# Queries and keys on both halves of the partitions: transposes on parts of the array in an attention and MLP kernel

## The chip, the cores and the metric

The kernel runs on one core of a Trainium2 chip. Its time is the device time of one execution in microseconds (us), beside it the profile of one more execution. The core has five engines that run side by side, each through its own instructions in order: TensorE (PE; its weight loads are PEld), VectorE (DVE), ScalarE (ACT), GpSimd (POOL) and SyncE (SP). POOL and SP issue all DMA transfers here. TensorE computes `out = in.T @ moving` with `in` as weights, and transposes by taking the tile as weights and an identity matrix as the moving operand. Results of TensorE lie in PSUM until VectorE or ScalarE copies them to SBUF.

## The reference

Inputs are q, k and v of 8 batches, 8 heads, 576 tokens, 64 values (float32), and two matrices `moe_w_in` (512 x 2048) and `moe_w_out` (2048 x 512). Per batch and head:

```python
scores = scale * np.matmul(q, k.transpose(0, 1, 3, 2))
mask_plain = (rel >= 0) & (rel < window)                 # heads 0 to 3, window 32
mask_dil = (rel >= 0) & (rel < window * dilation) & (rel % dilation == 0)   # heads 4 to 7, dilation 4
attn = softmax(where(mask, scores, -1e9));  out = attn @ v
x = out as (4608 tokens, 512);  h = x @ w_in;  result = silu(h) @ w_out
```

`rel` is the distance from a key's position to the query's. A query sees 32 keys: the last 32 positions, or every fourth of the last 128.

## The kernel before, in words

**Attention.** Heads come in two kinds, `z = 0` (heads 0 to 3, plain) and `z = 1` (heads 4 to 7, dilated). Scores and values work on blocks of 32 queries and 64 keys. For scores, q and k must lie transposed, head dimension on the partitions. For `z = 0` two heads share the 128 partitions (`qT`, `kT`). For `z = 1` the tokens are sorted into four classes (position modulo 4), and two neighbouring tokens, that is two classes, share the partitions (`qC`, `kC`).

**Loading.** `load_qk` (L89) brings q and k of one batch in by POOL, cast to f16, in four transfers: heads 0 to 3 of k and of q, then heads 4 to 7 of k and of q. Partition p holds the tokens 8p to 8p + 7 of every head, so 72 partitions are in use. Batch 0 has a loader (`load_qk0`) and a transposer (`transpose0`) of its own, in two parts of the sequence.

**Transposing batches 1 to 7.** For `z = 0`, `pair` (L236) first copies two heads side by side on VectorE, so that one token's values of both heads are 128 neighbouring columns. `transpose` (L244) then makes eight transposes (one per token in the row) of 72 rows by 128 columns into one PSUM tile, and one copy sorts the result into `qT` or `kT`. For `z = 1` no pairing is needed, since two neighbouring tokens are neighbours in memory: `transpose_classes` (L257) makes eight transposes of the same size. For k the copy out of PSUM is made by VectorE, for q by ScalarE (`both`, L645). PSUM tiles with the tag `ps` rotate through four buffers.

**The MLP.** `layer1` (L590) makes 16 blocks of hidden units, each of 8 matmuls (288 columns), with SiLU on ScalarE; batch 0 does it in two parts (`layer1_part`). `layer2` (L623) makes 4 or 5 output tiles of 16 matmuls (512 columns).

**The order.** The schedule is written out by hand. `plan_of(b)` (L668) puts the attention work of later batches into batch b's MLP: `at(step, function, ...)` runs a function ahead of block `step` of layer 1 (0 to 15) or of a group of four matmuls of layer 2 (16 and up); negative steps belong to the first part of batch 0. The transposes of a batch and kind are made in two bursts, each for two head pairs' worth of one step: in batches 2 and later, `z = 1` of batch b + 1 at steps 2 and 6, `z = 0` of batch b + 2 at steps 12 and 14, with the pair copies at 9 and 10, and scores follow at steps 10 and 17. `load_qk(b + 3)` is issued at step 8. In the start, POOL's order is: q and k of batch 0, v of batch 0, `w_in`, q and k of batch 1, `w_out`, the clearing of a v buffer, v of batch 1, q and k of batch 2. SyncE shifts v of batch 1 (`shift_v`) from step 14 of batch 0 on.

## Time and profile before

| | |
|---|---|
| median of 3 runs | 344.65 us (343.04 to 346.63) |
| the profiled execution | 345.1 us, of which the span of instructions is 343.3 us |
| granted TensorE clock | 1.0 throughout |
| TensorE busy | 320.1 us (93%), 4824 matmuls |
| VectorE busy | 194.1 us (57%) |
| ScalarE busy | 216.6 us (63%) |
| POOL busy | 76.4 us (22%) |
| layer 1 of batches 1 to 7 (L595) and layer 2 (L631) | 119.1 + 132.2 us of TensorE |
| transposes of batches 1 to 7 (L253, L262) | 224 of `z = 0` and 224 of `z = 1`, in 28 bursts of 16 |
| q and k transfers of batches 1 to 7 (L96) | 28 of 288 KB |

How to read the profile: an operation's line names the engine, the line of the kernel, what it writes and reads, its shape (for TensorE rows*columns of the weights first) and its count. Matmuls are pipelined: the length of one includes its way through the array, so the distance between starts tells what it costs. A row of slices shows 40 equal slices of the span, each digit the busy share in tenths. The chain of waits follows the last instruction back to what released it.

### The profile page before, as it was taken

Reading aid. Unit: us, or ns where it says so; the run is one execution under the profiler, and the core shown is the slowest. Engines: PE = TensorE matmul, PEld = TensorE weight load, DVE = VectorE, ACT = ScalarE, POOL = GpSimd, SP = SyncE. Lnnn points to the kernel's source line nnn. Section 1 sums busy time; section 2 is a strip of 40 time slices with the busy share of each in tenths; the row PEclk is TensorE's granted clock in tenths of the full one; section 3 lists DMA queues with packets and bytes.
Section 4 is the critical chain, followed back from the end, with each engine's and each line's share of the span. In section 5 each row is a group of like instructions: output and inputs, shape, how many; then the busy total and the mean of one; then the engine's idle time right before and its main releaser. Section 6 shows DMA issues by size and latency. Waiting matters only on the chain.

```text
span 343.3 us, 11208 instructions
## 1 busy us (share of the span) xinstructions
PE 320.1 (93%) x4824; PEld 209.5 (61%) x4824; DVE 194.1 (57%) x438; ACT 216.6 (63%) x746; POOL 76.4 (22%) x120
## 2 busy tenths in 40 slices
PE   4549998799999999999899999999999999999995
PEld 4437863377744677467655677458755677457642
DVE  7776575866667755855656456655756443440021
ACT  2693669046799556976499356986599356916400
POOL 8835543254200450044001530023000000000000
PEclk9999999999999999999999999999999999999999
DMA  6999999989911596158802946039002100110021
GB/s 85 165 215 189 202 190 179 215 155 113 144 62 50 94 128 101 63 77 121 138 7 89 161 80 96 33 82 137 10 5 91 63 2 3 61 63 2 0 83 71
DMA packets 49089, 32.84 MB, mean 96 GB/s; under 512 B 24112, under 2 KB 43568, under 8 KB 49040
## 3 DMA queue, kind: packets, MB, share of 16 engines
q0 software_dynamic: 42848, 21.74, 47.6%
q1 hardware_dynamic: 6192, 10.39, 9.2%
q8 instruction: 37, 0.61, 0.7%
q14 instruction: 12, 0.10, 0.1%
HBM read 37.75 MB, written 9.44 MB: 137 GB/s over the span
## 4 chain that ended last, share of the span: by engine, by line
PE 73%; DMA 16%; ACT 3%; DVE 3%; issue 2%; POOL 1%; SPq 0%; POOLq 0%
PE h L595 33%; PE o L631 28%; DMA w_out<-in_moe_w_out_dram 5%; DMA vw<-in_v_dram 4%; PE x L507 3%; ACT pe L446 3%; DMA vw<-vw 3%; DMA w_in<-in_moe_w_in_dram 2%; PE pt L471 2%; DMA qn<-in_q_dram 2%; PE t L253 2%; PE t L262 2%; DVE pn L462 1%; PE s L306 1%; PE s L294 1%
## 5 line engine op out<-in xcount | busy, mean ns | idle before, releaser
L631 PE MATMUL o<-w_out,gT 128*128 128x512 f16 x576 | 132.2, 380 | 0.0
L603 ACT ACTIVATE gT<-h 128x576 f16<-128x576 f32 x112 | 72.8, 650 | 85.0 <-PE h L595 85.0
L595 PE MATMUL h<-xT,w_in 128*128 128x288 f16 x896 | 119.1, 287 | 1.3 <-issue 1.3
L595 PEld LDWEIGHTS <-w_in 128*128 128x128 f16 x896 | 84.4, 98 | 23.5 <-issue 1.7
L446 ACT ACTIVATE pe<-ms,nm 128x64 f32<-128x64 f32 x284 | 94.2, 334 | 3.3 <-DVE nm L375 3.2
L631 PEld LDWEIGHTS <-gT 128*128 128x128 f16 x576 | 53.8, 98 | 58.0
L639 DVE COPY ob<-o 128x512 f32<-128x512 f32 x36 | 24.8, 689 | 59.1 <-PE o L631 59.1
L446 ACT ACTIVATION_READ_ACCUMULATOR pe<-ms,nm 128x1 f32 x284 | 53.2, 187 | 0.0
L402 DVE SCALAR_TENSOR_TENSOR ms<-s,mask 128x512 f32<-128x512 f32 x28 | 19.2, 686 | 26.3 <-PE ss L294 17.6
L119 POOL DMA_DIRECT2D vw<-in_v_dram x16 | 10.2, 639 | 103.1 <-PE xs L564 98.6
L586 DVE CAST xT<-x 128x256 f16<-128x256 f32 x56 | 21.1, 418 | 12.4 <-PE xs L553 8.2
L462 DVE TENSOR_TENSOR pn<-pe,r 128x640 f16<-128x640 f32 (+2 forms) x32 | 25.3, 792 | 1.1
L418 DVE TENSOR_REDUCE nm<-ms 128x10 f32<-128x640 f32 (+1 forms) x28 | 22.0, 786 | 1.0
L479 DVE COPY ptT<-pt 128x640 f16<-128x640 f16 (+2 forms) x32 | 15.0, 470 | 11.5 <-PE pt L471 11.5
L614 PE MATMUL h<-xT,w_in 128*128 128x256 f16 (+1 forms) x128 | 19.4, 304 | 0.8 <-DVE xT L543 0.8
L269 DVE COPY kC<-t 128x576 f16<-128x576 f16 (+2 forms) x18 | 12.3, 686 | 12.2 <-PE t L262 12.2
L471 PE MATMUL pt<-ident,pn 128*128 128x128 f16 x152 | 14.7, 229 | 4.5 <-DVE pn L462 4.5
L621 ACT ACTIVATE gT<-h 128x512 f16<-128x512 f32 (+1 forms) x16 | 10.4, 650 | 11.6 <-PE h L614 11.6
L471 PEld LDWEIGHTS <-pn 128*128 128x128 f16 x152 | 10.1, 101 | 12.1 <-DVE pn L462 9.7
L507 PEld LDWEIGHTS <-vw 64*64 64x64 f16 x896 | 9.7, 109 | 11.2 <-issue 10.0
L255 DVE COPY kT<-t 128x576 f16<-128x576 f16 x14 | 10.5, 754 | 8.3 <-PE t L253 8.3
L614 PEld LDWEIGHTS <-w_in 128*128 128x128 f16 x128 | 12.5, 103 | 4.3 <-issue 0.8
(82 smaller groups left out, 288.9 us busy)
## 6 DMA issues: line engine op xcount, KB each, us to landing
out_dram<-ob SPq DMA_DIRECT2D x36, 256.0 KB, 2.0
kn<-in_k_dram POOLq DMA_DIRECT2D x14, 288.0 KB, 8.6
qn<-in_q_dram POOLq DMA_DIRECT2D x14, 288.0 KB, 9.1
vw<-in_v_dram POOLq DMA_DIRECT2D x8, 288.0 KB, 6.7
vw<-in_v_dram POOLq DMA_DIRECT2D x16, 128.0 KB, 3.6
w_in<-in_moe_w_in_dram POOLq DMA_DIRECT2D x4, 512.0 KB, 12.0
w_out<-in_moe_w_out_dram POOLq DMA_DIRECT2D x4, 512.0 KB, 17.2
vw<-vw POOLq DMA_DIRECT2D x12, 128.0 KB, 2.7
```

Source lines behind the costliest of these rows:

```text
L402: nc.vector.scalar_tensor_tensor(out=ms[:, 0:8].rearrange("p (n t) c -> p n (t c)", n=2), in0=s[hi].rearrange("p n t c -> p n (t c)"), sca ...
L418: nc.vector.tensor_reduce(out=nm[:, 0:w], in_=ms[:, 0:w], axis=AX.X, op=ALU.max, negate=True)
L446: nc.scalar.activation(pe[:, t, :], ms[:, t, :], AF.Exp, bias=nm[:, t : t + 1], accum_out=l[:, t : t + 1],)
L462: nc.vector.tensor_tensor(pn[:, 0:w], a["pe", z, hi][:, 0:w], r[:, 0:w, None].broadcast_to([P, w, KB]), ALU.mult)
L471: nc.tensor.transpose(t[:, i, :], a["pn", z, hi][:, 2 * i : 2 * i + 2].rearrange("p t c -> p (t c)"), ident)
L507: nc.tensor.matmul(dst, w, p, start=True, stop=True)
L586: copy(f(xT[:, 2 * z + n, 0:NS]), f(a["x", z][n]))
L595: nc.tensor.matmul(h[:, half, 0:HS], w_in16[:, c, f * P : f * P + P], xT[:, c, half * HS : half * HS + HS], start=(c == 0), stop=(c == MC ...
L603: nc.scalar.activation(gT[:, f, s0 : s0 + S].rearrange("p (a c) -> p a c", a=2), h[:, :, 0:HS], AF.Silu)
L614: nc.tensor.matmul(h[:, i, 0 : c1 - c0], w_in16[:, c, (f + i) * P : (f + i + 1) * P], xT[:, c, c0:c1], start=(c == 0), stop=(c == MC - 1),)
L631: nc.tensor.matmul(o, gT[:, f, t * P : (t + 1) * P], w_out16[:, f, :], start=(f == 0), stop=(f == NFF - 1),)
L639: nc.vector.tensor_copy(ob, o)
```

## The change

- `load_qk` puts the heads of a batch on both halves of the partitions. For `z = 0`, heads 0 and 1 lie on partitions 0 to 63 and heads 2 and 3 on 64 to 127, with 9 tokens per partition. For `z = 1`, heads 4 and 5 lie on partitions 0 to 47 and heads 6 and 7 on 64 to 111, with 12 tokens per partition. There are eight transfers per batch (two heads each) in place of four, `z = 1` ahead of `z = 0`.
- `pair` and its buffers are gone.
- `transpose` now makes a burst for all four heads of a kind of q or of k. For `z = 0` it has 9 x 2 x 2 = 36 transposes of 64 rows by 64 columns, each on a quarter of the array: the half of the partitions gives the rows, the head within the pair the columns. For `z = 1` it has 6 x 2 x 2 = 24 transposes of 48 rows by 128 columns, on a half of the array. The two halves write two PSUM tiles; both are copied out at the end of the burst, one by VectorE and one by ScalarE.
- The steps of the bursts stay; one burst is for k and the next one for q, where each had one head pair's k and q before. Batch 0 keeps its transposes in parts, in tiles of the new names.

```diff
+HF = P // 2
+URS = (9, 12)
     def load_qk(b):
-        qk[b] = (
-            nat.tile([UP, H, UR, D], F16, tag="qn", name=f"qn_{b}"),
-            nat.tile([UP, H, UR, D], F16, tag="kn", name=f"kn_{b}"),
-        )
-        for h0 in (0, HH):
-            for dst, src in ((qk[b][1], k), (qk[b][0], q)):
-                nc.gpsimd.dma_start(
-                    out=dst[:, h0 : h0 + HH],
-                    in_=src[b, h0 : h0 + HH].rearrange("h (p u) d -> p h (u d)", u=UR),
-                )
+        for which in (0, 1):
+            t = nat.tile([P, H * UR, D], F16, tag=f"n{which}", name=f"n{which}_{b}")
+            u0, u1 = 2 * URS[0], 2 * (URS[0] + URS[1])
+            qk[b, 0, which] = t[:, 0:u0].rearrange("p (h u) d -> p h u d", h=2)
+            qk[b, 1, which] = t[:, u0:u1].rearrange("p (h u) d -> p h u d", h=2)
+        for z in (1, 0):
+            for which, src in ((1, k), (0, q)):
+                for i in (0, 1):
+                    h = 2 * (2 * z + i)
+                    nc.gpsimd.dma_start(
+                        out=qk[b, z, which][i * HF : i * HF + UPS[z]].rearrange("p h u d -> p h (u d)"),
+                        in_=src[b, h : h + 2].rearrange("h (p u) d -> p h (u d)", u=URS[z]),
+                    )
...
-    def pair(b, hp, which):
-        a = att(b)
-        p = a["pair", hp, which] = prp.tile([UP, UR, 2, D], F16, tag="pair", name=f"p{which}_{b}_{hp}")
-        nc.vector.tensor_copy(
-            p, qk[b][which][:, 2 * hp : 2 * hp + 2].rearrange("p h u d -> p u h d")
-        )
-    def transpose(b, hp, which, copy=nc.vector.tensor_copy):
...
+    def transpose(b, z, which, copies):
+        a = att(b)
+        src, n, ur = qk[b, z, which], UPS[z], URS[z]
+        ts = [ps.tile([P, ur, n], F16, tag="ps", name=f"t{which}_{b}_{z}_{i}") for i in (0, 1)]
+        for u in range(0, ur, 1 + z):
+            for h in (0, 1):
+                for i in (0, 1):
+                    r = slice(i * HF, i * HF + n)
+                    if z == 0:
+                        dst, w = ts[i][h * D : h * D + D, u, :], src[r, h, u, :]
+                    else:
+                        dst = ts[i][:, u // DIL * 4 + 2 * h + u % DIL // 2, :]
+                        w = src[r, h, u : u + 2, :].rearrange("p u d -> p (u d)")
+                    nc.tensor.transpose(dst, w, ident[r, r])
+        for i in (0, 1):
+            if z == 0:
+                o = (a["qT"][:, i], a["kT"][:, i, W:])[which]
+                copies[i](o.rearrange("d (p u) -> d p u", u=ur), ts[i].rearrange("d u p -> d p u"))
+            else:
+                to_classes(a, which, i, 0, ts[i].rearrange("d (e m) p -> d e m p", m=4), copies[i])
...
-    both = (nc.scalar.copy, nc.vector.tensor_copy)
+    both = (nc.vector.tensor_copy, nc.scalar.copy)
+    def transposes(at, b, z, steps):
+        for n in (0, 1):
+            at(steps[n], transpose, b, z, 1 - n, both)
...
-            transposes(at, 1, 0, (1, 1, 3, 3), (-2, -2, -1, -1))
+            transposes(at, 1, 0, (1, 3))
...
-                transposes(at, b + 1, 1, (2, 2, 6, 6))
+                transposes(at, b + 1, 1, (2, 6))
...
-                transposes(at, b + 2, 0, (12, 12, 14, 14), (9, 9, 10, 10))
+                transposes(at, b + 2, 0, (12, 14))
```

More of the change, by code (lines that the diff above doesn't have):

```diff
@@ L46 @@
     CL = S // DIL
-    UP = S // UR
+    UPS = [S // u for u in URS]
     HS = S // 2
@@ L51 @@
     PA = SA // UR
+    PB = (S - SA) // UR
     WM = 12
@@ L57 @@
     nat = ctx.enter_context(tc.tile_pool(name="nat", bufs=2))
-    prp = ctx.enter_context(tc.tile_pool(name="prp", bufs=4))
     msp = ctx.enter_context(tc.tile_pool(name="msp", bufs=5))
@@ L89, in load_qk, with load_qk0 @@
     def load_qk(b):
-        qk[b] = (
-            nat.tile([UP, H, UR, D], F16, tag="qn", name=f"qn_{b}"),
-            nat.tile([UP, H, UR, D], F16, tag="kn", name=f"kn_{b}"),
-        )
-        for h0 in (0, HH):
-            for dst, src in ((qk[b][1], k), (qk[b][0], q)):
-                nc.gpsimd.dma_start(
-                    out=dst[:, h0 : h0 + HH],
-                    in_=src[b, h0 : h0 + HH].rearrange("h (p u) d -> p h (u d)", u=UR),
-                )
-    def load_qk0(part, halves):
-        t0, n = ((0, PA), (SA, UP - PA))[part]
-        if part not in qk0:
-            qk0[part] = (
-                nat.tile([UP, H, UR, D], F16, tag="qn", name=f"qn_0{part}"),
-                nat.tile([UP, H, UR, D], F16, tag="kn", name=f"kn_0{part}"),
-            )
+        for which in (0, 1):
[11 more added lines that the diff above has]
+                    )
+    def load_qk0(part, halves):
+        t0, n = ((0, PA), (SA, PB))[part]
+        if part not in qk0:
+            qk0[part] = [
+                nat.tile([P, H * UR, D], F16, tag=f"n{i}", name=f"n{i}_0{part}").rearrange(
+                    "p (h u) d -> p h u d", h=H
+                )
+                for i in (0, 1)
+            ]
         for h0, h1 in halves:
@@ L160, in class_v @@
         return a["vw"][e * KB : e * KB + KB, NP + j // 2 * ND + h * DIL + r]
-    qk = [None] * B
+    qk = {}
     qk0 = {}
@@ L234, in att @@
         return state[b]
-    def pair(b, hp, which):
+    def transpose(b, z, which, copies):
         a = att(b)
-        p = a["pair", hp, which] = prp.tile([UP, UR, 2, D], F16, tag="pair", name=f"p{which}_{b}_{hp}")
-        nc.vector.tensor_copy(
-            p, qk[b][which][:, 2 * hp : 2 * hp + 2].rearrange("p h u d -> p u h d")
-        )
-    def transpose(b, hp, which, copy=nc.vector.tensor_copy):
-        a = att(b)
-        if hp >= HP // 2:
-            return transpose_classes(b, qk[b][which], 0, UP, hp, which, copy)
-        t = ps.tile([P, UR, UP], F16, tag="ps", name=f"t{which}_{b}_{hp}")
-        p = a.pop(("pair", hp, which))
-        for u in range(UR):
-            nc.tensor.transpose(t[:, u, :], p[:, u], ident[:UP, :UP])
-        o = (a["qT"][:, hp], a["kT"][:, hp, W:])[which]
-        copy(o.rearrange("d (p u) -> d p u", u=UR), t.rearrange("d u p -> d p u"))
@@ L257, in transpose_classes @@
-    def transpose_classes(b, src, i0, n, hp, which, copy):
-        a = att(b)
-        t = ps.tile([P, UR // DIL, 4, UP], F16, tag="ps", name=f"t{which}_{b}_{hp}_{i0}")[:, :, :, 0:n]
-        for h in (0, 1):
-            for u in range(0, UR, 2):
-                nc.tensor.transpose(
-                    t[:, u // DIL, 2 * h + u % DIL // 2, :],
-                    src[0:n, 2 * hp + h, u : u + 2, :].rearrange("p u d -> p (u d)"),
-                    ident[0:n, 0:n],
-                )
-        dst, off = ((a["qC"], 0), (a["kC"], W))[which]
-        h0, i0 = 2 * hp - HH, off + i0
+        src, n, ur = qk[b, z, which], UPS[z], URS[z]
@@ new lines, in transpose, with to_classes @@
+        for i in (0, 1):
[4 more added lines that the diff above has]
+                to_classes(a, which, i, 0, ts[i].rearrange("d (e m) p -> d e m p", m=4), copies[i])
+    def to_classes(a, which, i, t0, t, copy):
+        e, n = t.shape[1], t.shape[3]
+        dst, i0 = ((a["qC"], 0), (a["kC"], W))[which]
+        i0 += t0 // DIL
@@ L269, in transpose_classes @@
         copy(
-            dst[:, h0 : h0 + 2, :, i0 : i0 + n * UR // DIL].rearrange("d h r (p e) -> d (h r) p e", e=UR // DIL),
+            dst[:, 2 * i : 2 * i + 2, :, i0 : i0 + n * e].rearrange("d h r (p e) -> d (h r) p e", e=e),
             t.rearrange("d e m p -> d m p e"),
@@ L277, in transpose0 @@
         src = qk0[part][which]
-        t0, n = ((0, PA), (SA, UP - PA))[part]
+        t0, n = ((0, PA), (SA, PB))[part]
+        t = ps.tile([P, UR, n], F16, tag="ps", name=f"t{which}_0{part}_{hp}")
         if hp >= HP // 2:
-            return transpose_classes(0, src, t0 // DIL, n, hp, which, copy)
-        t = ps.tile([P, UR, UP], F16, tag="ps", name=f"t{which}_0{part}_{hp}")[:, :, 0:n]
+            t = t.rearrange("d (e m) p -> d e m p", m=4)
+            for h in (0, 1):
+                for u in range(0, UR, 2):
+                    nc.tensor.transpose(
+                        t[:, u // DIL, 2 * h + u % DIL // 2, :],
+                        src[0:n, 2 * hp + h, u : u + 2, :].rearrange("p u d -> p (u d)"),
+                        ident[0:n, 0:n],
+                    )
+            return to_classes(a, which, hp - HP // 2, t0, t, copy)
         for u in range(UR):
@@ L641, in layer2 @@
             nc.sync.dma_start(out=out[row : row + P, :], in_=ob)
-    both = (nc.scalar.copy, nc.vector.tensor_copy)
-    def transposes(at, b, z, steps, pairs=None):
-        for n in range(4):
-            hp, which = 2 * z + n // 2, 1 - n % 2
-            if z == 0:
-                at(pairs[n], pair, b, hp, which)
-            at(steps[n], transpose, b, hp, which, both[which])
+    both = (nc.vector.tensor_copy, nc.scalar.copy)
+    def transposes(at, b, z, steps):
+        for n in (0, 1):
+            at(steps[n], transpose, b, z, 1 - n, both)
     def later(at, b, z, steps):
@@ L693, in plan_of @@
             at(-3, last_finish, 0, 0, 1)
-            transposes(at, 1, 0, (1, 1, 3, 3), (-2, -2, -1, -1))
+            transposes(at, 1, 0, (1, 3))
             at(5, scores, 1, 0)
-            transposes(at, 1, 1, (7, 7, 9, 9))
+            transposes(at, 1, 1, (7, 9))
             at(10, load_qk, 3)
@@ L710, in plan_of @@
             at(0, shift_v, 3, nc.gpsimd, (ALL,))
-            transposes(at, 2, 0, (2, 2, 4, 4), (0, 0, 2, 2))
-            transposes(at, 2, 1, (8, 8, 10, 10))
-            transposes(at, 3, 0, (14, 14, 15, 15), (11, 11, 12, 12))
+            transposes(at, 2, 0, (2, 4))
+            transposes(at, 2, 1, (8, 10))
+            transposes(at, 3, 0, (14, 15))
             at(6, scores, 2, 0)
```

## The prediction

> **What bounds the kernel now.** I read the page first: the engines' busy time, the row of slices and the chain.

> ```profile
> PE 320.1 (93%) x4824; PEld 209.5 (61%) x4824; DVE 194.1 (57%) x438; ACT 216.6 (63%) x746; POOL 76.4 (22%) x120
> ...
> PE   4549998799999999999899999999999999999995
> ...
> PE 73%; DMA 16%; ACT 3%; DVE 3%; issue 2%; POOL 1%; SPq 0%; POOLq 0%
> ```

> TensorE is busy in nearly every slice after the first four. The answer by stretches sharpens that: from 113 to 306 us it is idle for 1.6 us of 193, while VectorE, which the change relieves, is idle for 81.

> ```profile
> 113.00:306.00 193.00, 191.39 (x2905) 125.09 (x2897) 112.37 (x252) 132.89 (x453) 31.33 (x48) 1.00 0.41 74
> ```

> Then the waits of TensorE, to see whom it waits for. After 25 us there are few: for the softmax rows `pn`, for the shifted v once, and 1.29 us at 166.5 that nothing in the profile explains ("issue").

> ```profile
> PE pt L471 <- DVE pn L462: 4.5, 8, 1.3
> ...
> PE x L507 <- DMA vw<-vw: 1.1, 1, 1.1
> ```

> So almost all of the change must be read from how long TensorE's stream becomes. Its timeline shows the bursts in the stream (columns: start, length with the pipeline's tail, operation, count; the distance of starts is what a burst costs).

> ```profile
> 200.75 0.43 PE L262 MATMUL t<-ident,kn 72*128 72x72 f16 x8
> 201.01 0.43 PE L262 MATMUL t<-ident,qn 72*128 72x72 f16 x8
> 201.27 1.15 PE L595 MATMUL h<-xT,w_in 128*128 128x288 f16 x8
> 202.35 0.43 PE L507 MATMUL x<-ptT,vw 64*64 64x32 f16 x32
> 202.63 0.21 PE L553 MATMUL xs<-ptT,vw 64*64 64x32 f16 x4
> 202.77 1.15 PE L595 MATMUL h<-xT,w_in 128*128 128x288 f16 x8
> ...
> 306.46 15.84 PE L595 MATMUL h<-xT,w_in 128*128 128x288 f16 x128
> 322.14 17.43 PE L631 MATMUL o<-w_out,gT 128*128 128x512 f16 x80
> ```

> Sixteen old transposes cost 201.27 - 200.75 = 0.52 us, 32 ns each, and nothing is lost going into or out of them: they use the whole array as the layers do. The 128 matmuls of layer 1 give 15.68 / 128 = 0.1225 us each, so the eight from 201.27 end at 202.25. The values burst on quarters of the array (64*64) starts at 202.35 and the layer goes on at 202.77: 36 small matmuls cost 0.52 us in all. In the trace's single starts each quarter takes its next matmul every 32 ns and the four run side by side: nine rounds, 0.29 us, and so 0.23 us for entering and leaving the quartered array. That burst is the nearest row to the new transposes.

> **What it removes.** 28 copies that put heads side by side, four per batch:

> ```profile
> L240 DVE COPY p<-kn 72x1024 f16<-72x1024 f16 x14 | 6.0, 429 | 0.0
> ...
> L240 DVE COPY p<-qn 72x1024 f16<-72x1024 f16 x14 | 6.0, 425 | 0.0
> ```

> That is 12.0 us of VectorE. I cost it at nothing: TensorE's dense stream covers it. The `pn` waits are not behind these copies: at 100.1 VectorE had itself waited for ScalarE's exponentials (1.8 us), and at 67.0 the chain is the sum of `pe`, two casts and `pn`; the pair copies of that stage begin at 71.9. Without the cover each copy would be worth 0.42 us. One small stall may go: a burst at 211.5 cost 0.69 instead of 0.52, four matmuls in. I take -0.15, between -0.2 and 0.

> **What it adds on TensorE.** Each batch had four bursts of 16; it now has two of 36 (heads 0 to 3, 64 rows by 64 columns of weights, 64 columns streamed) and two of 24 (heads 4 to 7, 48 rows by 128, 48 streamed), at the same steps. Seven batches make 14 of each.

> Heads 0 to 3: nine rounds over four quarters. Weights of 64 columns gave the 32 ns round of the values. A stream of 64 columns shows in the scores, where four matmuls on different tiles start every 29 ns, so the longer stream does not set the round. 9 x 0.032 + 0.23, and 13 ns for the longer last stream, is 0.53 against 0.52: 14 x 0.01 = +0.15 us. From below: 0.51, no change. From above, rounds in which load and stream add up (27 + 29 ns): 0.73, +3 us. I stay with the values' row, which has this tile and this order of banks.

> Heads 4 to 7: a stream of 72 costs 32 ns and one of 128 costs 56 (five `pt` in 0.28 us), so 48 cost 22. Twelve rounds with both halves side by side: 0.26 + 0.23 = 0.49, 14 x -0.03 = -0.4 us. The bound above with halves in parallel is the weight load of 128 columns, at most 16.5 ns: at the start, where `pt` takes 105 ns instead of 56, transposes on 40 rows follow each other every 33 ns.

> ```profile
> 12.43 0.43 PE L262 MATMUL t<-ident,kn 40*128 40x40 f16 x8
> 12.70 0.43 PE L262 MATMUL t<-ident,qn 40*128 40x40 f16 x8
> ```

> 24 such loads in turn are 0.40 + 0.23 = 0.63: +1.5 us. With no switch to pay: 0.26, -3.6 us. I take 0.49, since both the values and the scores pay the switch and both run the two halves of the rows in parallel.

> The copies out of PSUM stay: two per burst, one on VectorE (0.76 us) and one on ScalarE (0.63), of 576 columns as before. They start up to 0.26 us later, when the whole burst is done; the scores come 1.2 us or more after the burst's end, so nobody waits. Both PSUM tiles must be free at the start of a burst instead of one after the other: at most 0.26 us, against a slot freed about a microsecond earlier.

> **What it moves on the queues.** Each batch's q and k are eight transfers of 144 KB instead of four of 288: POOL spends some 8 x 0.6 (a 128 KB issue costs 0.58 to 0.64 us) instead of 4 x 0.73, +1.9 us per batch; it is 22% busy. Behind them stand w_out, the clearing of v, v of batch 1 and the next q and k. POOL's waits show that an issue waits for the landing of the transfer eight before it: w_out's first issue, at 20.84, waited for w_in. It will now wait for the first piece of k, which I expect about 31.5. The queue has work until 37, so it does not run dry, and v of batch 1, landing at 52.35, keeps its place. The transfers on 72 partitions post four of their sixteen completions about 2.6 us before the other twelve when the queue is quiet (86.65 against 89.25 to 89.77); 64 and 48 partitions should spread evenly. Bytes are the same and rows fewer (896 instead of 1152 per batch). If v lands sooner, the 1.1 us wait at 61.75 shrinks, but VectorE's chain to the `pt` at 67.03 follows only 0.5 us. So -0.5 to 0 here.

> The order turns round: heads 4 to 7 first, heads 0 to 3 last, though the latter are wanted first, at 36.94 (k) and 38.55 (q). By the landing records of before, the third and fourth quarter of the load land at 36.34 and 37.23; these become heads 0 to 3, so margins are 0.6 and 1.3 us. If the queue slips by 2 us it costs up to 1.5 us. For all of the start I take -0.2, from -0.5 to +1.5.

> **Sum**, against the profiled execution (345.1 us, span 343.3 and 1.8 around it): +0.15 - 0.4 - 0.15 - 0.2 = -0.6, so 344.5. The median of the runs, 344.65, lies 0.45 below that execution, so 344.1.

> **The rivals.**
> - *Halves in turn*: if the two row halves do not stream together when the weights span all 128 columns, 24 x 22 ns + 0.23 = 0.76, +0.24 x 14 = +3.3 us: 347.7. If the quarters' rows take turns as well, 18 x 32 + 230 = 0.81 us, +4 more: 351.7. This is the slower side; it costs from a round of two above 24 ns on, and passes 1% by itself at 46. For it: no burst of before has 64*128 tiles in both halves. Against: values and scores share rows side by side.
> - *Loads wait for streams*: if a weight load could not run beside a stream in the same rows, a round of heads 0 to 3 would hold two loads (27 ns each: 64-column pairs follow every 53 ns at the start's half pace) and two streams (29): 9 x 0.112 + 0.23 = 1.24, +10 us; heads 4 to 7, 12 x (16.5 + 22) + 230 = 0.69 us, +2.4: 356.9. Against: in the values burst a quarter's load starts 2 ns after its own stream (203.943 after 203.941) and the next stream comes 31 ns later; in turn they would need 40.
>  [...]
> - *VectorE frees TensorE*: if the waits after 25 us for `pn` (0.86, 0.47, 1.32, 0.49, 0.30, 0.25, 0.27) and for v (1.1) all went, -5.1: 339.4. For it: 12 us less work on the engine that makes `pn`. Against: the chains above.
> - *Late loads*: heads 0 to 3 of batch 1 land after 36.94 and TensorE stands: +1.5, 345.9.

> **How the numbers follow.** Forecast 0.62, halves in turn 0.17 (0.10 for heads 4 to 7 alone, 0.07 for both), loads wait 0.04, VectorE 0.10, late loads 0.07. About 1% is what a measurement can tell from no change: 3.4 us. Slower by more: 0.07 + 0.04, half of the 0.10, and 0.02 for sums of small losses, 0.18. Faster: 0.10. The rest, 0.72, is within 1%. The range goes from halfway to the VectorE case, 340.8, to above the case of 347.7, 348.4, and leaves out 0.07 + 0.04 above and about half of 0.10 below. The forecast's own range, with the start's bounds, the loads in turn and one unexplained 1.29 us more or less, is 342.0 to 347.0.

> **What would show it.** Bursts of 36 at about 0.53 us and of 24 at about 0.49; VectorE's busy time near 182; POOL near 90; batch 1's first transposes still at about 37 us; no new wait at `t`. I am wrong if 24 transposes take over 0.65 us, if TensorE waits for `n1` or `n0` after 25 us, or if the waits for `pn` vanish.

## The result, and the profile after

| | before | after |
|---|---|---|
| median of 18 runs each, us | 345.31 (342.92 to 347.47) | 348.25 (346.37 to 349.39) |
| ratio of the times | | 1.0087 (95%: 1.0068 to 1.0106) |
| profiled execution, its span, us | 345.1, 343.3 | 348.6, 346.8 |
| mean granted clock in the profile | 1.000 | 0.995 |

The changed kernel is slower by 0.9%, 2.9 us, where the forecast was 0.6 us less. Its page has these lines in place of those shown of before; the last but one is the queue that the profile calls instruction, with packets, MB and share.

```profile
PE 321.5 (93%) x5216; PEld 203.4 (59%) x5216; DVE 184.6 (53%) x410; ACT 216.4 (62%) x746; POOL 88.3 (25%) x148
...
PE   4549899889999999999999999999999999999995
...
PEclk9999989999999999999999999999999999999999
...
q8 instruction: 41, 0.67, 0.8%
...
PE 76%; DVE 8%; DMA 6%; ACT 5%; issue 2%; POOL 1%; SPq 0%; POOLq 0%
```

A slice is 8.67 us. The clock's row has one that isn't full, the sixth (43.4 to 52.0 us), and ahead of it, in the fifth slice, TensorE's digit has fallen from 9 to 8: that is the place. The long middle is no worse than before: TensorE is idle for 0.95 us of the same 193, before it was 1.6.

```profile
113.00:306.00 193.00, 192.05 (x3118) 121.17 (x3117) 107.78 (x236) 137.35 (x479) 36.43 (x60) 1.00 0.41 74
```

In TensorE's waits one line is new, the second. The third has taken the place of the wait for the shifted v.

```profile
PE pt L483 <- DVE pn L474: 5.2, 8, 1.3
...
PE s L306 <- issue: 2.1, 1, 2.1
...
PE x L519 <- DVE xT L598: 0.7, 1, 0.7
```

The timeline shows where it stands, and what follows (start, length, operation, idle time before it in brackets):

```profile
38.03 0.48 PE L260 MATMUL t<-ident,n 64*64 64x64 f16 x36
38.44 1.26 PE L626 MATMUL h<-xT,w_in 128*128 128x320 f16 x8
39.63 0.48 PE L260 MATMUL t<-ident,n 64*64 64x64 f16 x36
40.04 1.26 PE L626 MATMUL h<-xT,w_in 128*128 128x320 f16 x8
...
41.29 0.68 PE L306 MATMUL s<-kT,qT 64*32 64x64 f16 x57
44.03 0.19 PE L306 MATMUL s<-kT,qT 64*32 64x64 f16 x1 [2.06 <-issue]
44.03 0.24 PE L306 MATMUL ss<-kT,qT 64*32 64x64 f16 x4
44.21 2.17 PE L626 MATMUL h<-xT,w_in 128*128 128x320 f16 x8
46.31 0.66 PE L260 MATMUL t<-ident,n 48*128 48x48 f16 x24
46.90 1.69 PE L626 MATMUL h<-xT,w_in 128*128 128x320 f16 x8
48.52 0.47 PE L260 MATMUL t<-ident,n 48*128 48x48 f16 x24
```

In the middle of the first scores of batch 1 TensorE stops for 2.06 us (2.26 from start to start), and no data that the profile knows of holds it. Then it is slow: eight layer matmuls take 46.31 - 44.21 = 2.10 us where the same eight from 40.04 took 1.19, the burst 0.59 instead of 0.41, the next eight 1.62. That is 0.91 + 0.18 + 0.43 = 1.5 us more. The granted clock is 0.5 from 44.40 to 47.81, 3.41 us, and 1.0 in the rest of its record up to the last matmul. The record begins at 30.7 us, in the profile of before at 30.5, so "1.0 throughout" in the table of before holds from there on: the eight layer matmuls of before from 25.51 took 1.66 us, the eight from 30.43 took 0.92. Stand and half clock are 3.7 us together.

Before had no stand at this place. It had one much later, the 1.29 us that the prediction calls unexplained:

```profile
40.31 0.69 PE L294 MATMUL s<-kT,qT 64*32 64x64 f16 x58
40.81 0.25 PE L294 MATMUL ss<-kT,qT 64*32 64x64 f16 x4
40.99 1.26 PE L614 MATMUL h<-xT,w_in 128*128 128x320 f16 x8
...
165.46 1.03 PE L595 MATMUL h<-xT,w_in 128*128 128x288 f16 x7
167.79 0.41 PE L595 MATMUL h<-xT,w_in 128*128 128x288 f16 x2 [1.29 <-issue]
```

To compare kernels I take two stretches of each profile: the *stage*, from the first 320-column matmul of batch 0's layer 1 to the first layer-1 matmul of batch 1; and the *rest*, from there to the last matmul. Ahead of the stage lie the start and the first part of batch 0's layer 1. Stage and rest are 33.66 and 268.07 us before, 37.35 and 266.85 after: +3.7 in the stage. Where layer 1 of batch 0 begins varies between executions whatever is changed (25.46 to 27.23 us among before and four experiments with the old transposes of batch 1, 25.68 to 26.99 among after and four with the new ones), so I don't read the 1.45 us by which it is later in this one.

Later bursts cost about what was forecast:

```profile
204.26 0.47 PE L260 MATMUL t<-ident,n 48*128 48x48 f16 x24
204.67 1.15 PE L607 MATMUL h<-xT,w_in 128*128 128x288 f16 x8
...
210.59 2.13 PE L607 MATMUL h<-xT,w_in 128*128 128x288 f16 x16
212.65 0.48 PE L260 MATMUL t<-ident,n 64*64 64x64 f16 x36
213.06 2.13 PE L607 MATMUL h<-xT,w_in 128*128 128x288 f16 x16
```

From a burst's start to the layer's next matmul are 0.41 us in both; with what the layer loses on the way in, 0.50 (0.503 for 36, 0.501 for 24, within 0.002 in 19 bursts; the old bursts of 16 by the same measure 0.52). In single starts a quarter takes its next transpose every 32 ns, as forecast, and a half every 25 ns, where 22 were forecast. 28 bursts save 0.5 us.

**What the trace has about the stand.** The packets of queue q8 are 16 KB each: 37 for the 9,648 matmuls and weight loads of before, 41 for the 10,432 of after. That is 261 and 254 instructions per packet; I take it for 256, an estimate: e5 below has stands after 1469 and after 1725, 256 apart. Counting matmuls and loads by their start in the trace gives this:

| | fifth 16 KB packet starts (instructions begun by then) and ends | instruction 1469 begins, the next one begins |
|---|---|---|
| before | 40.67 (1359), 41.65 | 43.8, no stand |
| after | 41.66 (1440), 42.55 | 41.77, 44.03 |

Rivals: the *loads* (eight transfers on fewer partitions) fill the DMA queues differently and hold something up; the *bursts* themselves cost time in every batch, in the array or by what their copies delay.

### The profile page after: what moved, and what is told of

The parts are those of the page before. It is cut to its first block, busy times and chain, and to the rows that moved or that the text cites. A ratio compares the mean times of both kernels' runs of the same rounds, so it can differ in the third digit from the quotient of the medians.

```text
span 346.8 us, 11988 instructions
## 1 busy us (share of the span) xinstructions
PE 321.5 (93%) x5216; PEld 203.4 (59%) x5216; DVE 184.6 (53%) x410; ACT 216.4 (62%) x746; POOL 88.3 (25%) x148
## 4 chain that ended last, share of the span: by engine, by line
PE 76%; DVE 8%; DMA 6%; ACT 5%; issue 2%; POOL 1%; SPq 0%; POOLq 0%
PE h L607 30%; PE o L643 27%; PE h L626 6%; ACT pe L458 4%; PE t L260 3%; PE x L519 3%; DVE pn L474 3%; PE pt L483 2%; DMA vw<-in_v_dram 2%; DMA vw<-vw 2%; DMA n<-in_k_dram 2%; ACT L458 1%; PE s L318 1%; DVE kC L273 1%; PE s L306 1%
## 5 line engine op out<-in xcount | busy, mean ns | idle before, releaser
L626 PE MATMUL h<-xT,w_in 128*128 128x256 f16 (+1 forms) x128 | 20.6, 317 | 0.8 <-DVE xT L555 0.8
L102 POOL DMA_DIRECT2D n<-in_q_dram x28 | 16.3, 592 | 15.5 <-DMA w_in<-in_moe_w_in_dram 5.5
L102 POOL DMA_DIRECT2D n<-in_k_dram x28 | 16.3, 591 | 10.4 <-DMA w_in<-in_moe_w_in_dram 3.6
```

Source lines behind the costliest of these rows:

```text
L102: nc.gpsimd.dma_start(out=qk[b, z, which][i * HF : i * HF + UPS[z]].rearrange("p h u d -> p h (u d)"), in_=src[b, h : h + 2].rearrange("h ...
L626: nc.tensor.matmul(h[:, i, 0 : c1 - c0], w_in16[:, c, (f + i) * P : (f + i + 1) * P], xT[:, c, c0:c1], start=(c == 0), stop=(c == MC - 1),)
```

## The experiments

All ratios are to the kernel before, run on the same chip beside them.

**1 to 4: which batch, which part.** `e1_old_first` keeps loads, pair copies and transposes of before for batch 1 and takes the new ones for 2 to 7; `e2_new_first_only` is the reverse.

```diff
+OLD = (1,)                  # e1;  e2: (2, 3, 4, 5, 6, 7)
+if b in OLD: load_qk_old(b), pair(...), transpose_old(...)
```

> Batch 1 is loaded and transposed in the old manner (72 partitions, pair copies, four bursts of 16), batches 2 to 7 in the new one. Theory A (TensorE runs out of instructions: the bursts of 72 and 48 instructions of batch 1 bring its stream to a block that has not been fetched while the DMA engines are full, it stands 2.06 us at the scores near 42 us, and the clock is granted at half for 3.4 us after that): no such stand, granted clock 1.000, the time within 1 us of before (344.3 to 345.8). Theory B (the new order and size of batch 1's loads delays the start, the stand at the scores is an accident of one run): also close to before, so this run does not tell A from B. Theory C (the new bursts themselves cost more than the old in every batch): 6/7 of the loss stays, near 347.9.

> The reverse: batch 1 in the new manner, batches 2 to 7 in the old one. Theory A: the stand of about 2 us at the scores near 42 us and the half clock after it are there, the whole loss and a little more (the later bursts' small gain is gone): 348 to 349.5, granted clock 0.993 to 0.996. Theory B: the same time, but without a stand at the scores in most runs, so a clock of 1.000. Theory C: 1/7 of the loss, 345.7.

`e3_loads_only` is the kernel before with eight transfers in the new order, still on 72 partitions:

```diff
-for h0 in (0, HH):
+for h0 in (HH, 0):
     for dst, src in ((qk[b][1], k), (qk[b][0], q)):
-        nc.gpsimd.dma_start(dst[:, h0 : h0 + HH], src[b, h0 : h0 + HH])
+        for h in (h0, h0 + 2):
+            nc.gpsimd.dma_start(dst[:, h : h + 2], src[b, h : h + 2])
```

> The kernel before with only the loads changed: eight transfers of two heads per batch, heads 4 to 7 ahead of heads 0 to 3, still on 72 partitions; transposes and pair copies as before. Theory A: within 0.7 us of before, granted clock 1.000. Theory B: the loss of the whole change, 347 to 348.5. Theory C: as before.

`e4_more_instr` is the kernel before with 80 more instructions in batch 1's plain bursts: 20 small transposes, whose results nobody uses, behind each burst of 16.

```diff
+if b == 1 and which == 0:
+    for u in range(20):
+        nc.tensor.transpose(t[:, u % UR, 0:8], p[0:8, u % UR], ident[0:8, 0:8])
```

> The kernel before with 20 more transposes (8 rows, 8 columns streamed, over values that are already there) behind each of batch 1's two bursts for heads 0 to 3: 80 more TensorE instructions ahead of the first scores of batch 1, as the change has, at some 0.5 us of work per burst, with loads and the rest as before. Theory A: 1 us for the work, and the stand at the scores near 43 us with the half clock after it, 348 to 350 in all, clock below 0.998. Theories B and C: 1 us for the work alone, 346.3, clock 1.000.

| | median, us | ratio (95%) | stage, us | rest, us |
|---|---|---|---|---|
| e1 | 345.32 | 1.0008 (0.9984 to 1.0032) | 33.59 | 268.98 |
| e2 | 348.26 | 1.0107 (1.0069 to 1.0145) | 37.72 | 268.10 |
| e3 | 344.55 | 1.0000 (0.9972 to 1.0028) | 33.50 | 266.46 |
| e4 | 348.51 | 1.0112 (1.0076 to 1.0149) | 35.55 | 268.22 |

The whole loss lies in batch 1's new loads and bursts; six batches of the new manner alone cost nothing that can be told, though e1's one profile has two more such stands, 1.8 us up to 95.1 and 0.9 us up to 135.6, in its rest. The loads are cleared as far as their number and order go (e3), not yet their partitions. e2's profile has the stand after the same instruction:

```profile
40.32 0.68 PE L346 MATMUL s<-kT,qT 64*32 64x64 f16 x57
43.41 0.19 PE L346 MATMUL s<-kT,qT 64*32 64x64 f16 x1 [2.40 <-issue]
```

The mean granted clock is 0.993 to 0.995 in all six timed runs of e2 and in 17 of 18 of after, and below 0.9965 in 4 of 100 of the kernel before; that is as 3.4 us at half clock make it (1.7 of 347); it is 1.000 in all twelve of e1. So stand and half clock are not the accident of one profile.

e4 hit the place and, with 348.51 us, the expected time, but not by the expected road. It makes the kernel before stop at the same scores, again after 1469:

```profile
42.62 0.68 PE L297 MATMUL s<-kT,qT 64*32 64x64 f16 x57
43.75 0.19 PE L297 MATMUL s<-kT,qT 64*32 64x64 f16 x1 [0.46 <-issue]
```

But its packet had ended at 42.48, before TensorE came there at 43.10, and TensorE waited for 0.46 us only, without half clock (0.998 to 1.000 in all six runs). Of its 1.9 us in the stage some 1.15 are the added transposes; two further waits of this kind, 0.7 and 1.6 us, follow at later blocks. Its median is 3.4 us above the kernel before, more than stage and rest of its one profile add up to (2.0); the profile's other 1.6 us lie ahead of the stage, where profiles of the same code differ too.

**5 and 6: the same instructions, later.** The first scores of batch 1 go from step 5 to step 9 or 7, behind other work.

```diff
-at(5, scores, 1, 0)
+at(9, scores, 1, 0)         # e6: at(7, ...)
```

> The changed kernel with the first scores of batch 1 moved from step 5 of batch 0 to step 9, two layer-1 groups (2.2 us) and one burst of 48 instructions later. Theory A (the stream of TensorE's instructions is not fetched in time): TensorE reaches the block's end near 44 us instead of 41.8, when the fetch is just through, so the stand shrinks from 2.1 to under 0.5 us and the half clock goes: 344.8 to 346, clock 0.998 or more. Theory D (the tiled bursts leave TensorE in a state in which the scores that follow stand, wherever they are): a stand of about 2 us stays, 348. What later scores cost VectorE and ScalarE is under 0.5 us.

> The same, moved to step 7 only, one layer-1 group (1.1 us) later. Theory A: the stand shrinks by those 1.1 us to about 1.0, too short for the half clock in most runs (the stand of 1.3 us in the profile of before left the clock at 1.0): 345.5 to 347. Theory D: no change, 348.

e5 took 347.10 us, ratio 1.0051 (1.0026 to 1.0075), e6 347.08, ratio 1.0049 (1.0020 to 1.0077); stages 36.87 and 35.98. Both lie above what the fetch theory expected (up to 346 and up to 347), and below the 348 of the theory that the scores stand wherever they are: some four tenths of the loss go. By the mean clock (0.994 to 0.995) the half clock came in 2 of e5's 12 timed runs and in 4 of e6's. The stand at 1469 shrinks, but in e5 the next block's end is now late, in the second scores:

```profile
43.51 0.49 PE L306 MATMUL s<-kT,qT 64*32 64x64 f16 x41 [0.59 <-issue]
...
44.81 0.45 PE L260 MATMUL t<-ident,n 48*128 48x48 f16 x23 [0.63 <-DVE ms L414]
...
49.98 0.39 PE L318 MATMUL s<-kC,qC 64*32 64x64 f16 x29 [1.57 <-issue]
```

1.57 us after 1725 = 6 x 256 + 189, and 0.6 us at a PSUM buffer that the moved scores still hold, which neither theory had named. e6 stands 1.00 and 0.62 us at the same two ends, and has the wait for the buffer as well.

**7: the same instructions, fewer transfers.** The changed kernel loads a quarter of `w_out` and sets the rest to zero on POOL, so its result leaves out three quarters of layer 2's weights. TensorE's instructions are all there.

```diff
 load_w_out(0)
-for c in range(1, 4): load_w_out(c)
+for c in range(1, 4): nc.gpsimd.memset(w_out16[:, 4 * c : 4 * c + 4, :], 0.0)
```

> The changed kernel with three quarters of w_out left out (set to zero by POOL instead of loaded), so that the DMA engines have 6 us less to do between 35 and 47 us. Theory A: the fetch near 38 us is served at once, no stand at the scores, clock 1.000, 344 to 345.8. Theory E (it is the pace of the instructions alone, whatever the DMA engines do): the stand stays, 347.5 to 348.5. POOL's 6 us of writing zeros delay v of batch 1 by less than the transfers left out save.

It took 343.89 us, ratio 0.9957 (0.9928 to 0.9986), stage 33.63. From 38 to 42 us the core's DMA engines move 40 GB/s, in after 209. In the pages' rows of the DMA engines' busy share (after, then e7) the fifth slice, which begins at some 34 us, falls from 9 to 5:

```profile
DMA  6999999939802199029901964039002100110022
...
DMA  6999599995611696149702982148001100110021
```

The fifth packet starts at 38.09, with 1254 instructions begun (in after: 41.66, 1440), and the scores run through but for 0.27 us, at number 1469 again:

```profile
39.73 0.94 PE L306 MATMUL s<-kT,qT 64*32 64x64 f16 x58
40.49 0.24 PE L306 MATMUL ss<-kT,qT 64*32 64x64 f16 x4
40.66 1.26 PE L626 MATMUL h<-xT,w_in 128*128 128x320 f16 x8
```

The stand of 2 us goes with the full DMA engines: from start to start it is 2.26 us at 209 GB/s and 0.27 at 40. Fewer transfers might speed other things too, so this alone doesn't show that it is the fetch.

**8, 11 and 12: more instructions, put earlier.** This is the sharpest test of the fetch theory: instructions added where TensorE waits anyhow move the ends of blocks to other places in the stream. e8 makes one burst of batch 0's transposes, at 9.5 us, seven times over (96 more); e11 and e12 put 48 and 64 small matmuls on zeros (96 and 128 instructions) into the first 4 us.

```diff
-for h in (0, 1):                                                       # e8
+for h in (0, 1) * (7 if (part, hp, which) == (1, 2, 1) else 1):
...
+junk = ps.tile([P, 512], F32, tag="ps")                                # e11; e12: 64
+for n in range(48):
+    nc.tensor.matmul(junk[0:D, 0:16], vws[0][0:W, NP], vws[0][0:W, NP + 1, 0:16])
```

> The changed kernel with 96 instructions more on TensorE, put where it is idle (48 repeated transposes between 9.5 and 12.1 us, while q of batch 0 is awaited). All later instructions move by 96 places against the blocks of 256 in which the stream is fetched. Theory A: the block's end falls at the beginning of the scores, its fetch is asked for about 2.5 us earlier, so the stand all but goes: 344.5 to 346, clock 0.998 or more, although the kernel does more. Theories D and E: unchanged, 348 to 348.5.

> The changed kernel with 96 instructions more on TensorE (48 small matmuls of zeros, unused) ahead of everything, in the 4 us in which it waits for the first k; the earlier kernel with 96 more put them at 9.5 us, where they ran past q's landing and cost the start 1.5 us. Theory A: no stand at the scores of batch 1 and no half clock, the start as in the changed kernel without them: 343.8 to 345.2, so faster than the changed kernel by 3 to 4 us and than the one before by up to 1. If the fetch is not the cause: 348.

> The same with 128 instructions (64 small matmuls). Theory A: the block's end comes just ahead of the first scores of batch 1, its fetch still earlier: 343.8 to 345.2 too. If it is not the cause: 348.

| | median, us | ratio (95%) | stage, us | rest, us |
|---|---|---|---|---|
| e8 | 345.83 | 1.0001 (0.9981 to 1.0022) | 33.73 | 266.80 |
| e11 | 344.96 | 1.0014 (0.9989 to 1.0038) | 33.57 | 267.17 |
| e12 | 346.42 | 1.0056 (1.0024 to 1.0089) | 34.55 | 268.37 |

The row of e12 leaves out one run of 350.33 us, whose mean clock was 0.994; the median of all twelve is 346.70. With 96 instructions more the changed kernel is faster, and the difference from before is no longer to be seen. Loads and bursts are those of after, so the partitions of the loads are cleared too. e11's scores:

```profile
40.36 0.69 PE L306 MATMUL s<-kT,qT 64*32 64x64 f16 x58
40.86 0.25 PE L306 MATMUL ss<-kT,qT 64*32 64x64 f16 x4
41.04 1.26 PE L626 MATMUL h<-xT,w_in 128*128 128x320 f16 x8
```

Its fifth packet started at 37.07 and ended at 37.97, long before TensorE came to 1469 at 40.38. Its clock is 0.998 to 1.000 in the timed runs. e12 was a miss: with 32 more the first stand is gone as well, but other block ends fall badly (1.05 us at 45.5, 0.82 at 135.7, 0.74 at 168.3, each 185 to 189 past a multiple of 256), and in the start TensorE idles for 1.66 us up to 11.31. The expectation of e11 puts e8's longer start down to q's landing; in e8's profile two such stands are there, 1.57 us up to 14.20 and 1.00 us up to 20.39.

**9 and 10: the later batches' loads.** q and k of batches 4 to 7 are loaded at step 18 instead of 8 or 11, when the fetches of the middle should find emptier queues; e9 on e8, e10 on the kernel before.

```diff
-at(8, load_qk, b + 3)
+at(18, load_qk, b + 3)
```

> The changed kernel with the 96 instructions in idle time, and with the loads of q and k from batch 4 on issued at step 18 (the long matmuls of layer 2) instead of steps 8 and 11, so that they no longer meet the dense bursts of steps 10 to 16. Theory A: the late fetches that stand or nearly stand near 90, 130 and 170 us come in time; what is left is the change's own gain of 0.02 us per burst: 344.0 to 345.2, faster than the kernel before by 0 to 1.3. If the late fetches cost nothing on the median: as the kernel with the 96 instructions, 345.8.

> The kernel before with the same loads moved to step 18 and nothing else. Theory A: its late fetches (the stand of 1.29 us near 166 in its profile) go, 344.0 to 345.2. If they cost nothing on the median: 345.3.

e9 took 346.42 us, ratio 1.0051 (1.0027 to 1.0075), a miss: nothing is gained behind the start (rest 266.83 against e8's 266.80). In the start, where its code is e8's, the stand after 1725 is 0.95 us long (0.50 in e8), and the first part of layer 1 takes 1.08 us more: the record of the full clock begins at 32.66 us there, in e8 at 30.14. e10 took 344.58, ratio 0.9997 (0.9973 to 1.0020). Its profile has a rest of 266.45 us, without before's 1.29 us stand, yet the median doesn't move: that stand in before's profile is not worth 1.3 us in its median.

**All block ends together.** Two more readings of the 14 traces explain the place and the length of the stands. The place: TensorE's stream also holds semaphore instructions, which the traces record: four (a drain among them) ahead of number 1469 and four more between 1725 and 2400. Counted with them, the remainders of 185 to 189 become one. TensorE idles by "issue" for more than 0.15 us 24 times in the 14 profiles, and each time it stops 193 past a multiple of 256, in the first 25 us too. The length: at *k* blocks and 193 the packet that bears on it is the *k*-th. At number 1469 that is the fifth:

| | fifth packet ends | TensorE begins number 1469 | the next one begins |
|---|---|---|---|
| e2 | 41.93 | 40.81 | 43.41 |
| after | 42.55 | 41.77 | 44.03 |
| e6 | 42.43 | 42.69 | 43.89 |
| e5 | 42.17 | 42.73 | 43.51 |
| e4 | 42.48 | 43.10 | 43.75 |
| e7 | 39.05 | 40.21 | 40.48 |
| before | 41.65 | 43.77 | 43.80 |

TensorE goes on 1.24 to 1.63 us after the packet's end in 23 of the 24 stands (1.82 in the other), however early it came. Of the 541 such block ends in the 14 profiles, the packet had ended less than 1.0 us ahead of TensorE, or had not ended yet, at 24, and these are the 24 stands; at the other 517 it had ended more than 1.0 us ahead. So e4's stand is short because e4 came 0.62 us after its packet's end, where after came 0.78 before it.

No version is faster than the kernel before, but for e7, which leaves work out.

## Why the prediction was wrong

- **The step that failed is "What it adds on TensorE".** It priced 784 more instructions by their time in the array alone. That time was right: 0.50 us per burst where 0.53 and 0.49 were forecast, -0.5 us where I had -0.25. The missing term, put at nothing without a reason, is, by the fetch theory, bringing them: 2.26 us of stand and 1.5 us of half clock at batch 1's first scores, +3.7 us, which less the 0.5 of the bursts leaves 3.2, near the 2.9 measured. Shown: the loss comes with batch 1's new loads and bursts alone (e1, e2), is not the split of the loads (e3), goes with the full DMA engines (e7: a stand of 0.27 us at 40 GB/s, in after 2.26 at 209), and goes when the stream's blocks are shifted (e8, e11). The link to the fetch rests on the packets' size and count, and on all 24 stands, which lie at one remainder of 256 and end within 0.4 us of one another behind their packets but for one; the trace names the queue, not what a packet holds.
- **Inside the burst two sizes were off and cancelled.** For heads 4 to 7 the forecast was 0.26 us of rounds and 0.23 for going in and out; the rounds of 25 ns make 0.30, which leaves 0.20.
- **The clue was there.** The text set aside 1.29 us at 166.5 as a wait that nothing in the profile explains, and put one such wait, more or less, into the forecast's own range. It was the same thing. So, by its place, was the small stall at 211.5 that the sum counts with -0.15 as one that goes with the pair copies: in before TensorE halts there for 0.2 us after number 6585, 193 past a multiple by the full count, 1.23 us after its packet's end. No run tests that term by itself.
- **No rival had this mechanism.** *Halves in turn* gave 347.7, close to the time, by another road: it needed bursts of 0.76 us, and they are 0.50. The range reached up to 348.4 for the sake of this rival, so it is luck that the measured 348.25 lies within it. *Loads wait for streams* (1.24 and 0.69 us) falls by the same rows.
- **What it removes**: the cost of nothing was right. VectorE's busy time falls by 9.5 us and no wait of TensorE goes with it (`pt` for `pn` 5.2 us, before 4.5), so *VectorE frees TensorE* falls too.
- **What it moves on the queues**: the cost was right, POOL's busy time grows by 11.9 us, 1.7 per batch. That v of batch 1 keeps its place was wrong: it landed at 49.59 instead of 52.35. Its wait of 1.1 us went, and as forecast little came of it: the next to be late is `xT`, 0.7 us.
- **Late loads**: did not happen; no transpose of batch 1 waits for its loads. But the start's full queues, which the text looked at for data alone, were the place.

**What stays open**: why the remainder is 193 and not 0 (63 instructions ahead of those in the trace would do it, which no trace shows); what the time between a packet's end and TensorE's next instruction is spent on; when a packet is asked for, so which block end will be late, which no theory here foretold in size for e9 and e12; why the record of the full clock begins anywhere between 28.7 and 32.7 us; and what the same stands in later batches are worth in the median.

## What to carry to other kernels

Ask of every burst of small instructions how fast TensorE gets through 256 instructions there, and how full the DMA engines are at that moment: here TensorE stood for 2.26 us behind 256 instructions in 3.5 us at 209 GB/s (after), for 0.27 at 40 (e7), and not behind 256 in 5.1 us at 207 (before; GB/s from 38 to 42 us). An idle time by "issue" in the middle of a dense stretch was a clue here, not noise: count all of TensorE's instructions up to it, semaphores included, see whether such stands share one remainder of 256, and when the instruction queue's packet ended. If so, put the dense burst where the queues are emptier, or shift the stream by instructions in a place where the engine waits anyhow (e8, e11: none at these scores); but a shift moves all later block ends as well, and with 32 more part of the loss came back (1.0056).

## What the runs showed of the hardware

- **Stands of 2.26 and 2.60 us were followed by half clock.** From start to start, the stands of after (2.26, of which 2.06 idle) and e2 (2.60, 2.40 idle) had 3.41 us at a granted clock of 0.5 behind them; those of 1.58 (before), 1.77 (e5), 1.80 (e1) and 1.84 us (e4) had none. The changes of the clock lie on steps of 3.413 us (in after the first stretch at full clock is 13.653, four of them, and the one behind the half clock 300.373, 88; in before the one stretch is 314.026, 92), and in both profiles the stand lay within one step: in after 40.98 to 44.40, and the clock fell at 44.40. Of the four shorter ones only e1's lay within one step. Whether a stand of that length across two steps would go free was not tried.
- **Tiles of the array ran side by side in both shapes of the new bursts.** 36 transposes on quarters (64 rows, 64 columns) and 24 on halves (48 rows, 128 columns) both cost 0.50 us. Four quarters start within 10 ns, every 32 ns, and two halves within 3 ns, every 25 ns: nine and twelve rounds are 0.29 and 0.30 us, so about 0.2 is for going in and out.
- **A stand of TensorE ended 1.24 to 1.63 us after its packet's end in queue q8**, in 23 of 24 stands of the 14 profiles; a packet that ended over 1.0 us ahead left no stand above 0.15 us at 517 block ends.
